# Packed products one half step later, from the third batch on, in a fused attention and feed-forward kernel

## The chip, the cores and the metric

One Trainium2 chip, one core of it. The metric is the device time of one launch in microseconds; the kernel before takes 954.0 us (median of 3 runs, 953.77 to 955.78). Lower is better.

## What is computed

Eight batches, 8 heads, 576 tokens, 64 columns a head, fp32. First an attention in two stages through 32 packed tokens, then a spectral mixing of its output and a feed-forward of width 2048:

```
s = 0.125 * p @ k.T ; a = softmax(s) ; p_packed = a @ v          # 32 x 64 a head
s = 0.125 * q @ p_packed.T ; a = softmax(s) ; x = a @ p_packed   # 576 x 64 a head
u  = x + real(fft(fft(x, axis=1), axis=2))                       # tokens, then 512 columns
un = (u - mean(u)) / sqrt(var(u) + 1e-6)
out = u + relu(un @ w_ch1) @ w_ch2
```

## The kernel before

The work has two halves that are laid into each other. `front(b)` computes `u` of one batch: it is a generator, cut by `yield` into pieces. `ffn` runs the feed-forward over a tile of four blocks of 128 tokens; there are nine tiles (0 to 8). During tile t the front of batch t+1 runs piece by piece between the matmuls of the feed-forward, and the last pieces of batch t (called `rest`: the tokens that a block has no place for, "the tokens apart", whose values are `px<-bd,fa`) run at its start.

A tile goes through 16 chunks j of the 2048 hidden columns. Each has an **up half** (12 matmuls of 512 columns into the PSUM buffer `ph`) and a **down half** (12 matmuls into `acc0` to `acc3`). After `ph` is full, ACT makes `hh` from it (relu, rounded high part, L964) and DVE makes `hl` (the low part, L965); both read `ph`. The down half that follows in the program belongs to the chunk before. Behind each half stands a call of `step(i)`:

```
up(j); step(2*j); down(j - 1); step(2*j + 1)
```

so that even steps stand behind an up half and odd steps behind a down half. `step` lets the next piece of `gen` (the front of the next batch) or of `rest` be issued there. On PE, DVE, ACT and POOL the instructions stand in the order in which this Python code issues them (a manual schedule); SP's DMAs are placed by the tool, save those that are pinned.

The pieces of a front and their order stand in `ORDER`, one string for batch 0, one for batch 1 and one for the others; `y` is a `yield`. Letters that matter here: S scores, D the scores sent to DRAM in blocks (`fare`) and back transposed (`e1T`, group 0 on SP's queue, group 1 on ACT's queue at step 2), X sums of the scores, p packed products (`po`), d transposes of the result (`pptp`, then `ppT`, `pph`, `ppl`), g spectrum of the packed values (`pg`, then `turned`), U queries against the packed keys (`s2Tt`, `s2T`), e subtraction of the maximum, m of the mean. The exponentials of e are issued one step after it, by `after(1, exps)` in `less_one`. A digit is the group of four heads, 0 or 1.

PSUM has eight buffers of 128 x 512: `acc0` to `acc3`, one named `ph`, three named `ps` that go round for all else. `queries(0, 1)` (L463) uses the buffer `ph` too, for the short tail of group 1:

```
tails = [bank("s2Tt")] + ([psf.tile([P, 512], F32, tag="ph", name="s2Tt")] if len(gs) == 2 else [])
```

`narrow` then issues the tails of both groups in turn (group 0 first), and the 512-wide parts after them. `packed(g)` (L425) multiplies `e1T` by the values and normalises with `rinv` on DVE (L439); `spread` on POOL makes `bd` of it. `Turned.send_next` sends a finished block of the next tile to DRAM and back, at the steps in `SENDS`, if its mean was taken in an earlier step.

Of the kernel before, what the change touches and what calls it, by code (L numbers as in the profile page):

```python
# [14 lines left out]
ALU = mybir.AluOpType  # L15
AX = mybir.AxisListType

P = 128
S = 576
HS = S // 2  # L20
D = 64
NPK = 32
# [19 lines left out]
         "i20 d1 w1 m0 q1 e1 T3 a0 f0 i120 g0 j0 r0 w2 w3 c0 w4 w5 i40 g1 m1 P0 w6 X0 j1 a1 f1 c1 r1 P1 X1 v2 W10 P2 w7 T2",  # L42
         "K0 K1 Q0 Q1 y S V0 V1 y X y p0 p1 y d0 d1 y g0 y U y g1 y e0 y e1 y y m0 y a0 y m1 y a1 y f0 y r0 y h0 y f1 y r1 y "
         "h1 y y",
         "V0 V1 S D y X Q0 Q1 y p0 p1 y d0 d1 y g0 y U y g1 y e0 y e1 y y m0 y a0 y m1 y a1 y f0 y r0 y h0 y f1 y r1 y "
         "h1 y y")


# [35 lines left out]
def tile_kernel(ctx, tc, kpT, qT, v, w1, w2, tabS, tabH, tabL, tabR, tabF, tabB, tabT, sel, ident_d, out):  # L84
    nc = tc.nc
# [14 lines left out]
    def bank(name):  # L100
        nbank[0] += 1
        if nbank[0] % 7 < 4 and spare:
            return psf.tile([P, 512], F32, tag=spare[nbank[0] % 7], name=name)
        return ps.tile([P, 512], F32, tag="ps", name=name)
# [115 lines left out]
    def load_weights(i):  # L220

        for _ in range(BITS[i]):
            bits(*topped.pop(0))
            fetch_free()
        for _ in range(TOPS[i]):
            tops(*coming.pop(0))
# [10 lines left out]
    now = {}  # L237
# [10 lines left out]
    def next_step():  # L248
        steps[0] = (steps[0] or 0) + 1
        for item in [x for x in due if x[0] <= steps[0]]:  # L250
            due.remove(item)
            item[1]()
# [39 lines left out]
    def front(b):  # L292
        kps, vts, qts, e1s, e1T, rinv, away = {}, {}, {}, {}, {}, {}, {}
# [8 lines left out]
        def in_place(kind, g, what):  # L302

            if b == 0:
                late[kind, g] = what
            else:
                what()
# [4 lines left out]
        def load_values(g):  # L312
            if b < 2:
                vt = load(v[b, :, g], [P, 5, 4 * D], "vt", (g, 4) if b == 0 else None, b == 1)
                vts[g] = [vt[:, c] for c in range(5)]
                return
            vt = load(v[b, :, g, 0:4], [P, 4, 4 * D], "vt", "wst", True)
            vts[g] = [vt[:, c] for c in range(4)]
            vts[g].append(load(v[b, :, g, 4], [P, 4 * D], "vt4", ("xh", "oh")[g], True))
# [51 lines left out]
        def chunk_rows(c):  # L371

            return P if c < 3 or b < 2 else P - 32
# [51 lines left out]
        def packed(g):  # L425

            if g not in vts:
                load_values(g)
            vt = vts[g]
            po = bank("po")  # L430
            for c in range(5):
                kk = chunk_rows(c)
                for h in range(4):
                    nc.tensor.matmul(  # L434
                        po[h * NPK:(h + 1) * NPK, :D], e1T[g][:kk, h, c, :],
                        vt[c][:kk, h * D:(h + 1) * D], start=(c == 0), stop=(c == 4),
                        tile_position=(0, h * NPK))
            pp2 = work.tile([P, 2, D], F32, tag="pp2", name="pp2")
            nc.vector.tensor_scalar(pp2, po[:, :D].unsqueeze(1).to_broadcast([P, 2, D]), rinv[g], None, ALU.mult)  # L439
            pp2s[g] = pp2  # L440

            def spread():
                mask, n = (bpair, 2) if b else (bmask, 4)
                bd[g] = work.tile([P, n, D], F32, tag=f"bd{n}", name="bd")
                nc.gpsimd.tensor_tensor(bd[g], pp2[:, 0:1, :].to_broadcast([P, n, D]), mask.unsqueeze(2).to_broadcast([P, n, D]),
                                        ALU.mult)

            in_place("b", g, spread)
# [158 lines left out]
        def folded_parts(g):  # L607
# [6 lines left out]

        parts = {"S": lambda _: scores(0, 1), "U": lambda _: queries(0, 1), "D": lambda _: scores_away(0, 1),
                 "s": scores, "t": turned_scores, "u": score_sums, "p": packed, "d": packed_parts, "q": queries, "e": less_one, "m": less_mean, "g": values_spectrum, "a": weights, "f": folded, "r": folded_rest,
                 "h": folded_parts, "c": copies,
                 "T": load_tables, "B": lambda _: load_turn(), "K": load_keys, "V": load_values,
# [173 lines left out]
        for t, base in enumerate((0, FO) if b else ()):  # L792
# [15 lines left out]
            h = work.tile([P, DM], F32R, tag="tmp", name="yr_h", bufs=3)  # L808
# [117 lines left out]
    def wsplits():  # L926

        for t, _ in enumerate(tiles):
            for n, j in [(0, 0)] + [x for j in range(1, NJ) for x in ((0, j), (1, j - 1))] + [(1, NJ - 1)]:
# [4 lines left out]
                yield  # L934

    def ffn(first, turned, step, nxt, alone):
        keys = turned.keys
        n = len(keys)
# [5 lines left out]
        def up(j, moves=(), between=lambda: None):  # L944
            moves = list(moves)
            wh, wl = ready.pop(0)

            pool, tag = (ps, "ps") if alone and j % 2 else (psf, "ph")
            ph = pool.tile([P, 512], F32, tag=tag, name="ph")

            step = T // 2 if first == 0 and j < SPL else T
            for t in (slice(i, i + step) for i in range(0, T, step)):
                for k in range(12):
                    if step < T:
                        c, (l, r) = k % 4, ((wh, uh), (wl, uh), (wh, ul))[k // 4]
                    else:
                        c, (l, r) = k // 3, ((wh, uh), (wh, ul), (wl, uh))[k % 3]
                    nc.tensor.matmul(ph[:, t], l[:, c * P:(c + 1) * P], r[:, c, t], start=(k == 0), stop=(k == 11))  # L958
                    if moves:
                        moves.pop(0)()  # L960
            between()
            hh = ffp.tile([P, 512], F32R, tag="hh", name="hh")
            hl = ffp.tile([P, 512], F32R, tag="hl", name="hl")
            nc.scalar.activation(hh[:, :T], ph[:, :T], AF.Relu)  # L964
            nc.vector.scalar_tensor_tensor(hl[:, :T], ph[:, :T], 0.0, hh[:, :T].bitcast(F32), ALU.max, ALU.subtract)  # L965
            return hh, hl
# [26 lines left out]
        for j in range(NJ):  # L993
# [13 lines left out]
            if nxt is not None and j == NJ - 2 and not nxt.sent:  # L1007
                less(0, 1)
            step(2 * j)
            sends(2 * j)  # L1010
            if nxt is None and j == NJ - 1:
# [77 lines left out]
    rest = gen0  # L1089
    for t, (first, tk) in enumerate(tiles):  # L1090

        gen = gens.pop(t + 1, None) or (front(t + 1) if t + 1 < B else iter(()))
        ended = []

        def step(i):

            next_step()
            if i == 2 and t + 1 < B and t:
                now.pop("back")()
            if i in ((1, 2) if t else (0, 2)):  # L1100
                next(rest, None)
            elif not ended and next(gen, None) == "rest":
                ended.append(gen)
            if t == 0:
                load_weights(i)
            assert i < 2 * NJ - 1 or t + 1 >= B or ended

        nxt = Turned(tiles[t + 1][1]) if t + 1 < len(tiles) else None

        with tc.manual_schedule(engines=MANUAL):  # L1110
            ffn(first, cur, step, nxt, t + 1 >= B)
        cur, rest = nxt, gen
# [114 lines left out]
```

## Time and profile before

| | |
|---|---|
| timed runs, median (range) | 954.0 us (953.77 to 955.78) |
| the profiled execution | 957.94 us, its span 956.1 us |
| mean granted TensorE clock | 0.994 |
| busy: PE, DVE, ACT, POOL | 940.9, 568.6, 444.5, 451.5 us |
| instructions | 15116 |

The profile is one execution, and it was longer than the timed runs. A busy time is the sum over the span in which an engine's datapath works; a row of the timeline has the start in us from the span's start, the duration in us, engine, line, operation, and what is written from what with shapes. A number in brackets behind a row is the time that the engine was idle before it, and what ended that. Matmuls are pipelined, so a row is longer than the distance to the next.

### The profile page before, as it was taken

The page shows a single profiled execution, that of the slowest core. Times are in us where ns is not written, and L with a number is a line of the kernel's source. Part 1 is how long each engine was busy: PE and PEld are TensorE (multiplying, and loading weights), DVE is VectorE, ACT ScalarE, POOL GpSimd, SP SyncE. Part 2 cuts the span into 40 slices and gives each one's busy share as a digit, 9 for nine tenths or more (in the row PEclk, how much of TensorE's full clock was granted, in tenths as well). Part 3 has the DMA queues.
Part 4 walks back from the last instruction along what each step waited for, and adds up shares of the span by engine and source line. Part 5 has one row for each costly group of instructions (what it writes and reads, how often), then busy time and mean ns, then how long its engine had stood idle before and what let it go on. Part 6 is the DMA issues. An engine that isn't in the chain of part 4 may idle for free.

```text
span 956.1 us, 15116 instructions
## 1 busy us (share of the span) xinstructions
PE 940.9 (98%) x5593; PEld 761.5 (80%) x5593; DVE 568.6 (59%) x1171; ACT 444.5 (46%) x909; POOL 451.5 (47%) x392
## 2 busy tenths in 40 slices
PE   8899999999999999999999999999999999999998
PEld 5678887788778887788778877888778878887886
DVE  6789866594648656684668476864668353123112
ACT  4698565434524444444534444454444443233231
POOL 4456444553445435543555354543554355444442
PEclk9899999999999999999999999999999999999999
DMA  9694226200440016200540045100610011001001
GB/s 353 239 328 132 68 88 194 81 1 1 150 142 26 1 46 210 85 1 24 167 149 1 1 133 176 55 1 23 212 34 19 20 48 45 23 23 45 1 0 45
DMA packets 49304, 81.00 MB, mean 85 GB/s; under 512 B 7120, under 2 KB 29136, under 8 KB 49232
## 3 DMA queue, kind: packets, MB, share of 16 engines
q1 hardware_dynamic: 42896, 69.82, 21.6%
q10 hardware_dynamic: 5328, 8.98, 2.9%
q0 software_dynamic: 1008, 1.25, 0.5%
q8 instruction: 44, 0.72, 0.3%
q14 instruction: 28, 0.23, 0.1%
HBM read 59.71 MB, written 20.32 MB: 84 GB/s over the span
## 4 chain that ended last, share of the span: by engine, by line
PE 93%; DVE 2%; DMA 2%; ACT 1%; POOL 1%; issue 1%; SPq 0%; ACTq 0%; DVEq 0%; POOLq 0%
PE acc L977 41%; PE ph L958 40%; PE px L693 2%; PE po L434 1%; DMA w1f<-w 1%; PE py L743 1%; DMA e1T<-fare 1%; PE py L289 1%; PE py L290 1%; PE py L288 1%; PE s2T L338 1%; PE s L338 0%; ACT e L365 0%; PE pz L635 0%; PE pz L658 0%
## 5 line engine op out<-in xcount | busy, mean ns | idle before, releaser
L110 POOL TENSOR_TENSOR wr_l<-w2f,wr_h 128x512 fp32r<-128x512 f32 x144 | 188.4, 1308 | 290.6 <-ACT wr_h L107 268.5
L110 POOL TENSOR_TENSOR wr_l<-w1f,wr_h 128x512 fp32r<-128x512 f32 x144 | 195.4, 1357 | 190.1 <-ACT wr_h L107 165.1
L965 DVE SCALAR_TENSOR_TENSOR hl<-ph,hh 128x512 fp32r<-128x512 f32 x144 | 99.5, 691 | 297.1 <-ACT hh L964 294.7
L977 PE MATMUL acc<-wr_h,hh 128*128 128x512 f32 x577 | 229.4, 398 | 0.0
L958 PE MATMUL ph<-uh,wr_h 128*128 128x512 f32 (+1 forms) x580 | 226.2, 392 | 1.0 <-ACT uh L107 1.0
L977 PE MATMUL acc<-wr_l,hh 128*128 128x512 f32 x577 | 226.3, 392 | 0.0
L977 PE MATMUL acc<-wr_h,hl 128*128 128x512 f32 x577 | 225.8, 391 | 0.0
L958 PE MATMUL ph<-ul,wr_h 128*128 128x512 f32 (+1 forms) x580 | 224.6, 389 | 0.5 <-DVE ul L110 0.5
L958 PE MATMUL ph<-uh,wr_l 128*128 128x512 f32 (+1 forms) x580 | 224.4, 389 | 0.0
L964 ACT ACTIVATE hh<-ph 128x512 fp32r<-128x512 f32 x144 | 86.1, 598 | 243.5 <-PE ph L958 243.2
L107 ACT CAST wr_h<-w1f 128x512 fp32r<-128x512 f32 x144 | 89.3, 620 | 185.2 <-POOL wr_l L110 80.3
L958 PEld LDWEIGHTS ph<-uh,wr_h 128*128 128x128 f32 x580 | 108.6, 188 | 29.0 <-DVE s L480 5.9
L977 PEld LDWEIGHTS acc<-wr_h,hh 128*128 128x128 f32 x577 | 108.8, 189 | 25.3 <-issue 1.6
L977 PEld LDWEIGHTS acc<-wr_h,hl 128*128 128x128 f32 x577 | 108.9, 189 | 23.1
L958 PEld LDWEIGHTS ph<-uh,wr_l 128*128 128x128 f32 x580 | 108.5, 188 | 22.6
L958 PEld LDWEIGHTS ph<-ul,wr_h 128*128 128x128 f32 x580 | 108.7, 188 | 21.9 <-DVE ul L110 1.0
L977 PEld LDWEIGHTS acc<-wr_l,hh 128*128 128x128 f32 x577 | 108.8, 189 | 21.1
L107 ACT CAST wr_h<-w2f 128x512 fp32r<-128x512 f32 x144 | 88.3, 613 | 33.1 <-PE acc L977 25.9
L1035 DVE SCALAR_TENSOR_TENSOR ubuf<-acc,stat,ubuf 128x512 f32<-128x512 f32 (+1 forms) x37 | 24.9, 731 | 2.1 <-PE acc L977 2.1
L262 ACT ACTIVATE junk<-ubuf,stat 128x512 f32<-128x512 f32 x36 | 25.8, 717 | 0.1
L266 POOL TENSOR_TENSOR stat<-stat,mhalf 128x1 f32<-128x1 f32 x36 | 25.7, 727 | 0.0
L613 DVE TENSOR_TENSOR fl<-f,fh 128x712 fp32r<-128x712 f32 x14 | 18.9, 1351 | 9.1 <-ACT fh L611 9.0
(222 smaller groups left out, 1084.7 us busy)
## 6 DMA issues: line engine op xcount, KB each, us to landing
kp<-kpT SPq DMA_DIRECT2D x16, 608.0 KB, 5.0
out<-ubuf SPq DMA_DIRECT2D x35, 256.0 KB, 3.9
far<-unt SPq DMA_DIRECT2D x28, 256.0 KB, 2.0
back<-far SPq DMA_DIRECT2D x112, 64.0 KB, 2.0
qt<-qT ACTq DMA_DIRECT2D x12, 576.0 KB, 5.1
vt<-v SPq DMA_DIRECT2D x12, 512.0 KB, 4.0
w1f<-w SPq DMA_DIRECT2D x9, 512.0 KB, 7.0
w2f<-w SPq DMA_DIRECT2D x9, 512.0 KB, 7.2
```

The lines of the kernel that those rows point to most:

```text
L107: copied = nc.scalar.copy(hi, src)
L110: (lo_eng or nc.vector).tensor_tensor(lo, src, hi.bitcast(F32), ALU.subtract)
L262: nc.scalar.activation(junk, u, AF.Square, bias=st[:, 1:2], scale=-sign, accum_out=st[:, 2:3])
L266: nc.gpsimd.tensor_tensor(st[:, 2:3], st[:, 2:3], mhalf, ALU.pow)
L288: nc.tensor.matmul(o, lh, rh, start=first, stop=False)
L613: nc.vector.tensor_tensor(fl[g], f, fh[g].bitcast(F32), ALU.subtract)
L693: nc.tensor.matmul(banks[r][rows, k * 256 + g * P:k * 256 + (g + 1) * P], x[g][at, w], bd[g][at].rearrange("p a d -> p (a d)"), start=True ...
L958: nc.tensor.matmul(ph[:, t], l[:, c * P:(c + 1) * P], r[:, c, t], start=(k == 0), stop=(k == 11))
L964: nc.scalar.activation(hh[:, :T], ph[:, :T], AF.Relu)
L965: nc.vector.scalar_tensor_tensor(hl[:, :T], ph[:, :T], 0.0, hh[:, :T].bitcast(F32), ALU.max, ALU.subtract)
L977: nc.tensor.matmul(acc[i][:, cols], l[:, w], r[:, cols], start=(j == 0 and k == 0), stop=(j == NJ - 1 and k == 2 and cols.stop == DM))
L1035: nc.vector.scalar_tensor_tensor(u[:, cols], acc[i][:, cols], stat_of[keys[i]][:, 2:3], u[:, cols], ALU.mult, ALU.add)
```

## The change

From the third batch on (b >= 2; tiles 1 to 6 carry such fronts):

- a `y` stands in front of `p0 p1`, so the packed products and all behind them come one half step later; a `y` behind `e1` goes, so that m0 and all behind it stay at their steps;
- both groups of the packed products go into one `ps` bank side by side, and are normalised after both;
- in every tile but the first, the last piece of `rest` (the values of the tokens apart) moves from step 2 to step 5, where it is issued ahead of the next piece of the front, which is `p0 p1`.

```
-         "V0 V1 S D y X Q0 Q1 y p0 p1 y d0 d1 y g0 y U y g1 y e0 y e1 y y m0 y a0 y m1 y a1 y f0 y r0 y h0 y f1 y r1 y "
+         "V0 V1 S D y X Q0 Q1 y y p0 p1 y d0 d1 y g0 y U y g1 y e0 y e1 y m0 y a0 y m1 y a1 y f0 y r0 y h0 y f1 y r1 y "
          "h1 y y")
...
-            po = bank("po")
+            if g == 0 or b < 2:
+                po = now["po"] = bank("po")
+            else:
+                po = now["po"]
+            po = po[:, g * D:(g + 1) * D]
...
-                        po[h * NPK:(h + 1) * NPK, :D], e1T[g][:kk, h, c, :],
+                        po[h * NPK:(h + 1) * NPK], e1T[g][:kk, h, c, :],
...
+            if b < 2:
+                normalized(g, po)
+            elif g == 1:
+                for k in range(2):
+                    normalized(k, now["po"][:, k * D:(k + 1) * D])
+
+        def normalized(g, po):
+
             pp2 = work.tile([P, 2, D], F32, tag="pp2", name="pp2")
-            nc.vector.tensor_scalar(pp2, po[:, :D].unsqueeze(1).to_broadcast([P, 2, D]), rinv[g], None, ALU.mult)
+            nc.vector.tensor_scalar(pp2, po.unsqueeze(1).to_broadcast([P, 2, D]), rinv[g], None, ALU.mult)
...
-            if i in ((1, 2) if t else (0, 2)):
+            if i in ((1, 5) if t else (0, 2)):
                 next(rest, None)
-            elif not ended and next(gen, None) == "rest":
+            if i not in ((1, 2) if t else (0, 2)) and not ended and next(gen, None) == "rest":
                 ended.append(gen)
```

`gen` isn't taken further at steps 1 and 2, as before. The pieces of the front then stand at: X Q 3, p 4 (now 5), d 5 (6), g0 6 (7), U 7 (8), g1 8 (9), e0 9 (10), e1 10 (11), m0 12 in both.

The order on PE in tile 3, at the packed products (`po`) and the values of the tokens apart (`px`). Before:

```order
L958 MATMUL ph<-uh,wr_l 128x512
L693 MATMUL px<-bd,fa 64x128 x4
L977 MATMUL acc_4034<-wr_h,hh 128x512
...
L958 MATMUL ph<-uh,wr_l 128x512
L434 MATMUL po<-vt,e1T 32x64 x16
L434 MATMUL po<-vt_4061,e1T 32x64 x4
L434 MATMUL po<-vt,e1T 32x64 x16
L434 MATMUL po<-vt_4065,e1T 32x64 x4
L977 MATMUL acc_4034<-wr_h,hh 128x512
```

And in the changed kernel (its lines are 12 higher from L450 on):

```order
L989 MATMUL acc_4035<-wr_h,hl 128x512
L705 MATMUL px<-bd,fa 64x128 x4
L438 MATMUL po<-vt,e1T 32x64 x16
L438 MATMUL po<-vt_4059,e1T 32x64 x4
L438 MATMUL po<-vt,e1T 32x64 x16
L438 MATMUL po<-vt_4063,e1T 32x64 x4
L970 MATMUL ph<-uh,wr_h 128x512
```

The values moved from behind an up half to directly ahead of the products, and both now stand behind a down half.

The order on PE in tile 3 at the queries (`s2Tt`, the tails, and `s2T`). Before:

```order
L977 MATMUL acc_4037<-wr_h,hh 128x512
L977 MATMUL acc_4037<-wr_l,hh 128x512
L977 MATMUL acc_4037<-wr_h,hl 128x512
L338 MATMUL s2Tt<-qt,ppT 32x64 x8
L338 MATMUL s2T<-qt,ppT 32x512 x8
L958 MATMUL ph<-uh,wr_h 128x512
```

And in the changed kernel:

```order
L970 MATMUL ph<-uh,wr_h 128x512
L970 MATMUL ph<-ul,wr_h 128x512
L970 MATMUL ph<-uh,wr_l 128x512
L338 MATMUL s2Tt<-qt,ppT 32x64 x8
L338 MATMUL s2T<-qt,ppT 32x512 x8
L989 MATMUL acc_4032<-wr_h,hh 128x512
```

The queries moved from behind a down half to behind an up half.

The order on DVE in tile 1 around the transposes of the queries, which read `s2Tt` and `s2T`. Before:

```order
L965 SCALAR_TENSOR_TENSOR hl<-ph,hh 128x512
L529 TENSOR_TENSOR turned<-pg,turn 128x516 x2
L535 TENSOR_TENSOR turned<-turned 128x258 x2
L480 STREAM_TRANSPOSE s_2157<-s2Tt 128x64
L480 STREAM_TRANSPOSE s_2156<-s2Tt 128x64
```

And in the changed kernel:

```order
L541 TENSOR_TENSOR turned<-pg,turn 128x516 x2
L547 TENSOR_TENSOR turned<-turned 128x258 x2
L977 SCALAR_TENSOR_TENSOR hl<-ph,hh 128x512
L492 STREAM_TRANSPOSE s_2166<-s2Tt 128x64
L492 STREAM_TRANSPOSE s_2165<-s2Tt 128x64
```

An `hl` now stands directly ahead of the transposes, where two sums of the spectrum stood.

## Rows read from the trace of the kernel before

**Rows 1.** The page: span, busy time and share of the engines, and the granted clock of TensorE in 40 slices, in tenths.

```profile
span 956.1 us, 15116 instructions
...
PE 940.9 (98%) x5593; PEld 761.5 (80%) x5593; DVE 568.6 (59%) x1171; ACT 444.5 (46%) x909; POOL 451.5 (47%) x392
...
PEclk9899999999999999999999999999999999999999
```

**Rows 2.** The waits of PE, longest first: engine, what waited, for what; us in total, times, longest us.

```profile
PE py L743 <- POOL f L592: 2.1, 1, 2.1
PE po L434 <- DMA e1T<-fare: 1.8, 1, 1.8
```

**Rows 3.** Timeline of PE in tile 2, packed products to the transposes behind them.

```profile
268.36 0.77 PE L434 MATMUL po<-vt,e1T 128*32 128x64 f32 x40
270.89 0.77 PE L434 MATMUL po<-vt,e1T 128*32 128x64 f32 x40 [1.76 <-DMA e1T<-fare]
271.59 0.66 PE L977 MATMUL acc<-wr_h,hh 128*128 128x512 f32 x1
...
276.04 0.38 PE L454 MATMUL pptp<-ident,pp 128*128 128x128 f32 x2
```

**Rows 4.** Two stretches in tile 2: start and end, length, busy us of PE, PEld, DVE, ACT and POOL (with instructions), then the granted clock, the DMA share and GB/s.

```profile
268.36:271.77 3.41, 1.65 (x82) 1.42 (x82) 1.00 (x3) 1.10 (x2) 1.95 (x3) 1.00 0.83 324
271.77:275.19 3.41, 3.41 (x9) 2.65 (x10) 1.40 (x3) 0.00 (x0) 0.57 (x1) 0.50 0.22 85
```

**Rows 5.** The chain that ended last, in tile 2: start, us, what.

```profile
266.14 4.35 DMA e1T<-fare
270.49 0.40 issue
```

**Rows 6.** Timeline of PE in tile 3, last matmul of an up half, packed products, down half, transposes, first matmul of the next up half.

```profile
375.33 0.39 PE L958 MATMUL ph<-uh,wr_l 128*128 128x512 f32 x1
375.79 1.33 PE L434 MATMUL po<-vt,e1T 128*32 128x64 f32 x80
377.05 0.50 PE L977 MATMUL acc<-wr_h,hh 128*128 128x512 f32 x1
...
379.94 0.38 PE L454 MATMUL pptp<-ident,pp 128*128 128x128 f32 x2
380.07 0.48 PE L958 MATMUL ph<-uh,wr_h 128*128 128x512 f32 x1
```

**Rows 7.** Timeline of PE, ACT and DVE behind three up halves. First the next work of PE, hh, the weight split behind it and hl in tile 3; then hl behind the up half of rows 6; then the next work of PE and hl in tile 2.

```profile
382.90 0.28 PE L521 MATMUL pg<-basis,pph 128*128 128x258 f32 x1
383.16 0.60 ACT L964 ACTIVATE hh<-ph 128x512 fp32r<-128x512 f32 x1 [1.51 <-PE ph L958]
383.66 0.61 ACT L107 CAST wr_h<-w2f 128x512 fp32r<-128x512 f32 x1
383.80 0.69 DVE L965 SCALAR_TENSOR_TENSOR hl<-ph,hh 128x512 fp32r<-128x512 f32 x1 [0.67 <-ACT hh L964]
...
376.38 0.69 DVE L965 SCALAR_TENSOR_TENSOR hl<-ph,hh 128x512 fp32r<-128x512 f32 x1 [1.84 <-ACT hh L964]
...
292.28 0.39 PE L977 MATMUL acc<-wr_h,hh 128*128 128x512 f32 x1
293.45 0.69 DVE L965 SCALAR_TENSOR_TENSOR hl<-ph,hh 128x512 fp32r<-128x512 f32 x1 [1.24 <-ACT hh L964]
```

**Rows 8.** Timeline of PE in tile 2, around the values of the tokens apart.

```profile
261.57 0.39 PE L958 MATMUL ph<-ul,wr_h 128*128 128x512 f32 x1
261.80 0.39 PE L958 MATMUL ph<-uh,wr_l 128*128 128x512 f32 x1
262.11 0.65 PE L693 MATMUL px<-bd,fa 64*64 64x128 f32 x8
262.70 0.50 PE L977 MATMUL acc<-wr_h,hh 128*128 128x512 f32 x1
263.04 0.40 PE L977 MATMUL acc<-wr_l,hh 128*128 128x512 f32 x1
```

**Rows 9.** All hh and all hl of the span: count, duration in ns (min/median/max), first and last start.

```profile
L964 ACT ACTIVATE hh<-ph x144: 577/598/614, 47.9 to 946.4; 128x512 fp32r<-128x512 f32 x144
...
L965 DVE SCALAR_TENSOR_TENSOR hl<-ph,hh x144: 652/692/698, 48.5 to 947.0; 128x512 fp32r<-128x512 f32 x144
```

**Rows 10.** Timeline of DVE and PE in the first batch: a copy, and the matmuls that waited for it.

```profile
11.40 0.29 DVE L456 COPY ppT<-pptp 128x128 f32<-128x128 f32 x1 [0.42 <-PE pptp L454]
...
11.75 0.32 PE L338 MATMUL s2Tt<-w1f,ppT 64*32 64x64 f32 x8 [0.38 <-DVE ppT L456]
```

**Rows 11.** Timeline of PE in tile 3, the queries' wide parts and the next up half.

```profile
386.37 1.06 PE L338 MATMUL s2T<-qt,ppT 64*32 64x512 f32 x16
387.37 0.50 PE L958 MATMUL ph<-uh,wr_h 128*128 128x512 f32 x1
```

**Rows 12.** Timeline of ACT and DVE in tile 3: the squares of the tokens apart, both normalisations, and the high and low part of the packed values of group 0.

```profile
374.48 0.72 ACT L262 ACTIVATE junk<-ubuf,stat 128x512 f32<-128x512 f32 x1
...
377.05 0.60 DVE L439 TENSOR_SCALAR pp<-po,ri 128x128 f32<-128x128 f32 x2
...
380.57 0.27 ACT L107 CAST pph<-pptp 128x128 fp32r<-128x128 f32 x1
380.87 0.29 DVE L110 TENSOR_TENSOR ppl<-pptp,pph 128x128 fp32r<-128x128 f32 x1 [0.33 <-ACT pph L107]
```

## The prediction

> **What bounds the kernel now.** I read the page first: TensorE's share of the span and its granted clock [rows 1]. PE is busy for 940.9 of 956.1 us at full clock nearly throughout, so a saved microsecond of another engine is worth nothing unless PE waited for it, and every wait that is put on PE adds to the end. Then the list of PE's waits, longest first [rows 2]: the first, 2.1 us for a fold of the first batch, lies ahead of the tiles; the second is 1.8 us for scores that come back by DMA, and it is the one wait inside the tiles. Then the timeline of PE around that wait, in tile 2 [rows 3], the clock beside it [rows 4], the chain through it [rows 5] and the same place one tile later [rows 6]. Last I looked, on PE, ACT and DVE together, for whatever the moved pieces will newly meet: the end of an up half, where the bank "ph" is emptied [rows 7].
>
> **The DMA wait.** In tile 2 the packed products begin at 268.36, stop after the first group, and the second group starts at 270.89, after 1.76 us without work [rows 3]; the chain goes through the last return of e1T, which lands 0.40 us before that [rows 5]. From 271.77 to 275.19 the granted clock is 0.50, the lower of the two levels (1.2 GHz), after 1.00 in the stretch before [rows 4], so most of the down half behind the wait runs at half speed. In tile 3 the same two pieces run without trouble: packed products from 375.79 to 377.05, 1.26 us, down half to 379.94, 2.89 us [rows 6]. Tile 2 took 271.59 - 268.36 = 3.23 and 276.04 - 271.59 = 4.45 us [rows 3], so the wait with what the clock took cost 1.97 + 1.56 = 3.53 us. Tile 3 is just late too: its last up matmul starts at 375.33 and the products at 375.79, 0.46 us, where an interruption otherwise takes 0.31 [rows 6, 8], 0.15 us more. Together 3.7 us. With the products one half step (2.7 us) later, behind the down half, the second group in tile 2 would be asked for near 268.36 + 2.8 for the down half + 0.59 for the values [rows 8] + 0.63 for the first group (half of 1.26) = 272.4, some 1.5 us after the start that the data allowed. So 3.7 us of the profiled execution go. But this execution took 957.94 us and the median of the timed runs is 954.0: the 3.9 us between them are about this wait, so I take it that the timed runs mostly don't have it, and that it gives them nothing.
>
> **One interruption fewer.** A short piece put between full-width matmuls costs more than its own time. Around the values of the tokens apart, the step from the last up matmul to the piece is 0.31 us instead of 0.23, and the first step behind it is 0.34: 0.08 + 0.11 = 0.19 us [rows 8]. Now these 8 rows stand directly in front of the packed products, in tiles 1 to 6. One such pair goes, and one step from values to products comes, which the trace doesn't show: nothing at best, a full 0.19 at worst. The saving is 0 to 0.19 us a tile; I take the middle, 0.10, for both ends are equally near: 6 x 0.10 = 0.6 us, bounds 0 and 1.1. The Trainium skill, in TensorEngine Tiling (Array Packing), section Tiling Modes, says that a change of tiling mode drains the engine; values (64 x 64) and products (128 x 32) are two modes, so by it the new step isn't free and the saving would lie below the upper bound.
>
> **The queries land on a bank that is still being read.** This is the largest term. Everything behind the packed products moves one half step with them, so the queries (s2Tt, s2T) move from step 7 to step 8. Odd steps stand behind a down half, even steps behind an up half, as the order on PE shows. The tail of the second group is written into the only buffer "ph". At step 7 that buffer had been written one down half ago and emptied meanwhile. At step 8 it has just been filled, and the second matmul of the piece has to wait until ACT has made hh and DVE has made hl from it; in the order of DVE, hl now stands directly in front of the transposes of s2Tt. How long that is stands in tile 3: the first matmul behind the up half starts at 382.90, hh starts at 383.16, hl runs from 383.80 for 0.69 us and ends at 384.49 [rows 7], 1.59 us later. Both instructions are steady: hh 577 to 614 ns, hl 652 to 698 ns over 144 of each [rows 9]. From an end on DVE to the start of the matmul that waited for it takes 0.06 us (11.69 to 11.75, [rows 10]). PE takes matmuls in order, so the rest of the queries and the whole down half queue behind it: 1.65 us a tile, in tiles 1 to 6, 9.9 us. Nothing hides it, for PE has no slack. Below: the earliest end of hl in these rows is 376.38 + 0.69 - 375.79 = 1.28 us behind the up half, where PE itself came late [rows 6, 7]: 1.34 x 6 = 8.0. Above: where DVE or ACT came late, hl ended at 293.45 + 0.69 - 292.28 = 1.86 us [rows 7]: 1.92 x 6 = 11.5. I take 1.65, since that row is also the end of an up half with a short piece behind it. What the queries free in exchange is small: the next up half no longer follows directly on the transposes of s2Tt, but it didn't wait for them (s2T takes 1.00 us to the next up half, 386.37 to 387.37, the length of its own work, [rows 11]).
>
> **What else moves, at no cost on PE.** Both products share a bank and are normalised together: 0.60 us of DVE for the two [rows 12], behind DVE's sums of the tokens apart, which now stand there too; the transposes of the result come a whole up half later (380.07 to 382.90 is one, 2.83 us [rows 6, 7]), and that hides it. If it didn't, the transposes at step 6 would wait. Means: the exponentials of a group are issued one step before its means are taken, and have that half step on ACT; the steps from m0 on stay where they were. On SP the turned block of the tokens apart is sent at step 12 instead of 4 or 5 in tiles 1 and 3; it is split in the last steps, and behind it in that queue stand keys for the next tile. If that cover were gone, SP's transfers would come a few us later and still before the tile's end. The weight splits on POOL now pass the spread of the packed values one step later; they run a whole half step ahead of PE.
>
> **The sum.** Against the profiled execution: 957.94 - 3.7 - 0.6 + 9.9 = 963.5 us. Against the timed median, without the DMA wait: 954.0 - 0.6 + 9.9 = 963.3 us. I forecast 963.4 us. Its own ends are 954.0 - 1.1 + 8.0 = 960.9 and 954.0 + 11.5 = 965.5.
>
> **The rivals.** First, the clock falls after each new wait, as it did after the 1.76 us in tile 2 [rows 4]. Then the 1.56 us that it cost there come six times: 963.4 + 9.4 = 972.8 us; one, two or three times, 965.0 to 968.1. For it speaks that the new wait is nearly as long. Against it speaks the neighbourhood: in tile 2 the thin packed products lay on both sides of the wait and PE was busy for 1.65 of 3.41 us [rows 4], while now dense up matmuls end directly before it. The Trainium skill, in TensorE: Matmul & The Clock Gate, section "A second HAM failure mode: psum-queue depth-cycling", tells of a kernel that went round its PSUM banks and whose short idle times were enough to swing the clock between the levels; by that rule the time would be the 972.8 us above. No tile of this trace shows such a bank wait.
>
> Second, another wait comes beside it. At step 6 ACT now has hh, a weight split, the squares of the tokens apart and then the parts of the packed values, which the spectrum at step 7 multiplies. From the rows: hh from 0.26 us after the up half, the split from 0.76 to 1.37 [rows 7], squares 0.72 and, from the start of a part to the end of its low part on DVE, 380.87 + 0.29 - 380.57 = 0.59 [rows 12]: ready 2.7 us after the up half. PE comes there after two transposes, 0.13, and a down half of some 2.83, at 2.96 [rows 6, 7]. In tiles 1, 3 and 5, which have these squares, 0.3 us are left. If ACT comes a split (0.61 us) later, PE waits 0.3 us three times: 964.3 us.
>
> Third, on the other side: the new wait is short and the old one is worth its price in the timed runs too. This takes an hl that is done 0.93 us sooner than rows 7 say, since (3.7 + 0.6) / 6 = 0.72 us of wait a tile is the point at which it turns. Without any wait and with the DMA wait gone it would be 954.0 - 4.3 = 949.7 us, without the DMA wait in the timed runs 953.4. For it speaks that one timed run was 955.78, so waits of that kind come and go; against it, that hh and hl are two instructions in a chain, 0.58 + 0.65 = 1.23 us at their shortest [rows 9].
>
> **How the numbers follow.** Forecast 0.70, clock 0.15, second wait 0.07, other side 0.08. About 0.2% (1.9 us) is what a measurement of this kernel can tell from no change. The first three are slower by more than that: 0.92; the last is split evenly, 0.04 faster and 0.04 the same. The range goes from 960.5, just under the forecast's own lower end, to 969.6, which takes in a clock that falls after up to four of the six waits (963.4 + 4 x 1.56); outside stay the other side and the fullest clock cases, together some 0.15.
>
> **What would show it.** In the changed profile: the wait of the packed products for the DMA is gone, and they take 1.3 us in every tile; a wait of s2Tt for hl stands at the top of PE's list, 6 times, about 1.6 us each, always behind an up half; clock 1.00 in the tiles. The values of the tokens apart run straight into the products. If s2Tt doesn't wait, or waits under 0.7 us, the largest term is wrong; if low clock stands behind these waits, the first rival has it.

## The result and the profile after

The changed kernel takes 961.46 us (median of 6 runs, 961.2 to 961.98) against 954.12 us (6 runs, 953.36 to 955.78): ratio 1.007, 95% interval 1.006 to 1.008; by the medians it is 7.3 us slower. Forecast were 963.4 us, with 960.5 to 969.6 as the range.

The page of the changed kernel, to be read beside [rows 1]: the span grew by 3.1 us though PE is busy 2.8 us less. It grew by less than the timed 7.3 us because the profiled execution of the kernel before was a long one (957.94 us, with the DMA wait); that of the changed kernel took 961.2, as the timed ones do.

```profile
span 959.2 us, 15122 instructions
...
PE 938.1 (98%) x5593; PEld 760.1 (79%) x5593; DVE 566.4 (59%) x1171; ACT 444.4 (46%) x909; POOL 456.0 (48%) x392
...
PEclk9999999999999999999999999999999999999999
```

A 9 in the clock's row stands for 90% or more, so a fall of 3.4 us in a slice of 24 would not show in it. The stretch of a whole tile tells more (columns as in [rows 4]); here is tile 4:

```profile
467.30:571.88 104.58, 103.33 (x642) 83.86 (x641) 68.40 (x142) 46.72 (x98) 49.51 (x40) 1.00 0.24 78
```

The granted clock is 1.00, and so it is in the stretches of the tiles 1 to 3, 5 and 6; for the kernel before, the stretch of tile 2, with the fall of [rows 4] in it, shows 0.98.

PE's list of waits, beside [rows 2] (what waited, for what; us in total, times, longest):

```profile
PE s2Tt L338 <- DVE hl L977: 7.5, 6, 1.2
PE py L755 <- POOL f L604: 2.2, 1, 2.2
```

A wait that the kernel before did not have stands at the top, six times, once in each of the tiles 1 to 6. The wait of `po` for the DMA is gone from the list.

The queries in tile 3 on PE, ACT and DVE, beside [rows 7, 11]:

```profile
386.50 0.39 PE L970 MATMUL ph<-uh,wr_l 128*128 128x512 f32 x1
386.82 0.30 PE L338 MATMUL s2Tt<-qt,ppT 64*32 64x64 f32 x2
386.98 0.60 ACT L976 ACTIVATE hh<-ph 128x512 fp32r<-128x512 f32 x1 [2.85 <-PE ph L970]
387.61 0.69 DVE L977 SCALAR_TENSOR_TENSOR hl<-ph,hh 128x512 fp32r<-128x512 f32 x1 [1.48 <-ACT hh L976]
388.36 0.28 PE L338 MATMUL s2Tt<-qt,ppT 64*32 64x64 f32 x7 [1.25 <-DVE hl L977]
...
389.49 0.50 PE L989 MATMUL acc<-wr_h,hh 128*128 128x512 f32 x1
```

Read it downward: the tail of group 0 starts at 386.82, that of group 1 writes `ph` and has to wait for hl, which ends at 388.30; PE goes on at 388.36 and reaches the down half at 389.49. From 386.82 to 389.49 are 2.67 us. In the kernel before the same piece took 1.13, from its tails' row, here, to the up half at 387.37 of [rows 11]:

```profile
386.23 0.34 PE L338 MATMUL s2Tt<-qt,ppT 64*32 64x64 f32 x16
```

So the wait costs 1.54 us, though the list shows 1.25 for it: the list counts from the end of the matmul before.

The values of the tokens apart and the packed products, tile 4, beside [rows 6, 8]:

```profile
480.04 0.39 PE L989 MATMUL acc<-wr_h,hl 128*128 128x512 f32 x1
480.36 0.65 PE L705 MATMUL px<-bd,fa 64*64 64x128 f32 x8
480.94 1.34 PE L438 MATMUL po<-vt,e1T 128*32 128x64 f32 x80
482.21 0.50 PE L970 MATMUL ph<-uh,wr_h 128*128 128x512 f32 x1
```

Values 0.58 us and products 1.27 us, each as long as it was when it stood alone in front of a full-width matmul (0.59 in [rows 8], 1.26 in [rows 6]); the step from one to the other costs nothing more than that.

The length of a tile is the quickest measure of all that follows: from the first score matmul of tile 4 to that of tile 5, on PE. In this pair of tiles the profiled execution of the kernel before had no DMA wait. Before:

```profile
467.87 0.34 PE L338 MATMUL acc<-kp 64*32 64x64 f32 x15
...
571.14 0.34 PE L338 MATMUL acc<-kp 64*32 64x64 f32 x16
```

After:

```profile
467.30 0.32 PE L338 MATMUL acc<-kp 64*32 64x64 f32 x12
...
571.88 0.34 PE L338 MATMUL acc<-kp 64*32 64x64 f32 x15
```

103.27 us have become 104.58: 1.31 us more, which is 1.54 for the wait less 0.23 for the interruption saved (e3 below measures the 0.23 by itself). Six such tiles make 7.9 us.

### The profile page after: what moved, and what is told of

Same layout as the page of the kernel before. It is cut to its first block, busy times and chain, and to the rows that moved or that the text cites. A ratio compares the mean times of both kernels' runs of the same rounds, so it can differ in the third digit from the quotient of the medians.

```text
span 959.2 us, 15122 instructions
## 1 busy us (share of the span) xinstructions
PE 938.1 (98%) x5593; PEld 760.1 (79%) x5593; DVE 566.4 (59%) x1171; ACT 444.4 (46%) x909; POOL 456.0 (48%) x392
## 3 DMA queue, kind: packets, MB, share of 16 engines
q0 software_dynamic: 1008, 1.25, 0.5%
## 4 chain that ended last, share of the span: by engine, by line
PE 94%; DVE 2%; ACT 1%; DMA 1%; POOL 1%; issue 0%; SPq 0%; DVEq 0%; ACTq 0%; POOLq 0%
PE ph L970 41%; PE acc L989 41%; PE px L705 2%; PE po L438 1%; DMA w1f<-w 1%; PE py L289 1%; PE py L288 1%; PE py L290 1%; PE py L755 1%; PE s2T L338 1%; PE s L338 1%; PE pz L670 0%; DVE hl L977 0%; PE pz L647 0%; ACT hh L976 0%
## 5 line engine op out<-in xcount | busy, mean ns | idle before, releaser
L110 POOL TENSOR_TENSOR wr_l<-w1f,wr_h 128x512 fp32r<-128x512 f32 x144 | 199.2, 1383 | 185.3 <-ACT wr_h L107 158.0
L541 DVE TENSOR_TENSOR turned<-pg,turn 128x516 f32<-128x516 f32 x32 | 20.6, 688 | 11.7 <-PE pg L534 11.6
```

The costliest lines, as they stand in the source:

```text
L110: (lo_eng or nc.vector).tensor_tensor(lo, src, hi.bitcast(F32), ALU.subtract)
L541: nc.vector.tensor_tensor(x, pg[:, :N2].unsqueeze(1).to_broadcast([P, 2, N2]), w, ALU.mult)
```

## The experiments

All were timed in turn with the kernel before on their chip; the ratio is the one to compare, since its median there lay between 954.6 and 955.3 us. Where two rows are set against each other in microseconds, it is by what each lost to its own kernel before, by the medians. The tile is the one measured above.

| run | tile 4, us | time, us | ratio to before (95%) |
|---|---|---|---|
| kernel before | 103.27 | 954.12 | 1 |
| the change | 104.58 | 961.46 | 1.007 (1.006 to 1.008) |
| e1, queries at step 9 | 104.56 | 961.23 | 1.0071 (1.0058 to 1.0083) |
| e3, values at step 2 | 104.81 | 963.40 | 1.0090 (1.0076 to 1.0104) |
| e4, before, queries at step 8 | 104.82 | 963.45 | 1.0093 (1.0077 to 1.0109) |
| e6, wide parts first | 103.72 | 957.35 | 1.0023 (1.0014 to 1.0032) |
| e7, queries at step 7 | 103.03 | 953.06 | 0.9981 (0.9972 to 0.9990) |
| e8, e7 with values at step 2 | 103.26 | 954.53 | 0.9992 (0.9982 to 1.0001) |
| e9, before, values at step 4 | 103.67 | 957.11 | 1.0028 (1.0017 to 1.0040) |
| e10, e1 with gl on DVE | 107.74 | 977.54 | 1.0235 (1.0215 to 1.0255) |
| e11, before, values at 4, one bank | 103.04 | 954.52 | 0.9995 (0.9986 to 1.0004) |
| e12, the change with two banks | 104.66 | 964.52 | 1.0102 (1.0088 to 1.0116) |

**The place of the queries alone (e4).** One string of the kernel before is edited:

```
-         "V0 V1 S D y X Q0 Q1 y p0 p1 y d0 d1 y g0 y U y g1 y e0 y e1 y y m0 ..."
+         "V0 V1 S D y X Q0 Q1 y p0 p1 y d0 d1 y g0 y g1 y U y e0 y e1 y y m0 ..."
```

> The kernel before with one edit: the second spectrum at step 7 and the queries at step 8, behind an up half; packed products, values and means stay where they were. Theory: the wait for the bank comes alone, 6 x 1.54 = 9.2 us, 954.1 + 9.2 = 963.3 us. Rival (the loss comes from the late products): 954.1 us.

963.45 us, a tile of 104.82 (1.55 over), and PE's list has the new wait and no other in the tiles 1 to 6:

```profile
PE s2Tt L338 <- DVE hl L965: 7.5, 6, 1.2
```

The rival that late products cost by themselves falls: here they stand where they stood, and the loss is all there (8.1 us over the kernel before by the medians; 9.2 were expected).

**The wait made shorter (e6).** The wide parts of the queries are issued ahead of the tails (`wide` is true for the queries from the third batch on):

```
-            for c, w in ((1, slice(512, S)), (0, slice(0, 512))):
+            parts = ((1, slice(512, S)), (0, slice(0, 512)))
+            for c, w in reversed(parts) if wide else parts:
```

> The changed kernel with the 512-wide parts of the queries issued ahead of the tails, from the third batch on. Theory (the tail waits until hl has read ph): the wide parts, 0.99 us, run while hl is made, the wait falls from 1.54 to about 0.55 us, 6 x 0.99 = 5.9 us go: 955.5 us. Rival (the queries wait for something that comes with the step, such as the spectrum's banks or the packed values): the wide parts wait as the tails did, 961.5 us.

PE in tile 3:

```profile
385.71 1.09 PE L339 MATMUL s2T<-qt,ppT 64*32 64x512 f32 x16
386.60 0.27 PE L339 MATMUL s2Tt<-qt,ppT 64*32 64x64 f32 x2
387.25 0.34 PE L339 MATMUL s2Tt<-qt,ppT 64*32 64x64 f32 x14 [0.39 <-DVE hl L978]
387.52 0.50 PE L990 MATMUL acc<-wr_h,hh 128*128 128x512 f32 x1
```

The wide parts, in other banks, start at once, and the tail of group 1 still waits, now 0.39 us by its row: it is the bank `ph` that is waited for, nothing that the step brings. The piece takes 1.81 us instead of 2.67, 0.86 less (0.99 expected; the tails, issued last, now take longer at the end). A tile of 103.72 says the same. The run is 2.1 us over its kernel before where the change was 7.3 over, a gain of 5.3 us, as six times 0.86 = 5.2 asks; 5.9 were expected.

**The queries behind a down half again, later (e1).** In the changed kernel:

```
-         "... d0 d1 y g0 y U y g1 y e0 y e1 y m0 ..."
+         "... d0 d1 y g0 y g1 y U y e0 y e1 y m0 ..."
```

> The changed kernel with the queries one half step later again (step 9, behind a down half) and the second spectrum ahead of them at step 8. Theory (the loss is the wait of the queries' tail for the bank ph, and nothing else): the wait of s2Tt for hl is gone from PE's list, and 6 x 1.54 = 9.2 us go from 961.5, to 952.2 us, faster than the kernel before. Rival (the loss comes from the packed products and all behind them being late, wherever the queries stand): about 961 us, since here the queries are later still.

This missed. The queries no longer wait, as expected, but the time is that of the change, and so the number of the rival. The rival does not have it all the same: e4 above lost the time without late products, and e7 below has late products without the loss. PE's list names another wait:

```profile
PE ph L970 <- DVE s L492: 9.1, 6, 1.5
```

The up half behind the queries fills `ph` next, and it waits for DVE's transposes of the tail. PE, DVE and POOL in tile 4:

```profile
494.55 0.34 PE L338 MATMUL s2Tt<-qt,ppT 64*32 64x64 f32 x16
...
497.24 0.47 PE L970 MATMUL ph<-uh,wr_h 128*128 128x512 f32 x1 [1.50 <-DVE s L492]
```

```profile
494.04 2.90 DVE L547 TENSOR_TENSOR turned<-turned 128x258 f32<-128x258 f32 x2
496.86 0.37 DVE L492 STREAM_TRANSPOSE s<-s2Tt 128x64 f32<-128x64 f32 x2
```

```profile
493.92 1.30 POOL L110 TENSOR_TENSOR gl<-turned,gh 128x516 fp32r<-128x516 f32 x1
495.18 1.47 POOL L110 TENSOR_TENSOR wr_l<-w1f,wr_h 128x512 fp32r<-128x512 f32 x1
```

The two sums of the spectrum ahead of the transposes take 2.90 us (1.47 and 1.52, overlapping), with POOL at work without a gap beside them; the durations over all of them (count, shortest/median/longest in ns) are

```profile
L547 DVE TENSOR_TENSOR turned<-turned x28: 414/544/1522, 69.2 to 704.6; 128x258 f32<-128x258 f32 x28
```

and 420 to 430 ns over all in the kernel before. So the bank has two ends, and this order freed the one and shut the other. The theory stands in what it said of the queries' wait, and was too narrow in holding that nothing else could stop PE there.

**Is it POOL's work that slows the sums? (e10)** e1 with `TL = (0, 0, 1)`: the low parts `gl` of the later batches go from POOL to DVE.

> The run with the queries at step 9, with the low parts of the spectra (gl) made on DVE instead of POOL from the third batch on. There the sums of the second spectrum on DVE took 1.49 and 1.52 us beside POOL's work without a gap, 0.43 elsewhere, and the tail's transposes behind them came late. Theory (a DVE sum of two operands in SBUF is slow while POOL works): the sums fall to some 0.5 us, the wait of the up half for the transposes from 1.5 us to under 0.5 in spite of DVE's added 0.8, and the time falls by 5 us or more from 961.2. Rival (the transposes are late because of the place behind the spectrum): the wait grows by the added work to 2.3 us, 966 us.

977.54 us: neither theory's time. DVE in tile 4:

```profile
500.19 1.38 DVE L110 TENSOR_TENSOR gl<-turned,gh 128x516 fp32r<-128x516 f32 x1 [0.34 <-ACT gh L107]
501.49 1.28 DVE L541 TENSOR_TENSOR turned<-pg,turn 128x516 f32<-128x516 f32 x2
502.81 1.33 DVE L547 TENSOR_TENSOR turned<-turned 128x258 f32<-128x258 f32 x2
504.83 0.70 DVE L110 TENSOR_TENSOR gl<-turned,gh 128x516 fp32r<-128x516 f32 x1 [0.69 <-ACT gh L107]
```

The sums fell from 2.90 to 1.33 us with less work on POOL, and the same `gl` takes 1.38 us at 500.19, where POOL made a weight split (499.71 to 501.01), and 0.70 at 504.83, where POOL was idle. POOL beside them:

```profile
499.71 1.30 POOL L110 TENSOR_TENSOR wr_l<-w2f,wr_h 128x512 fp32r<-128x512 f32 x1 [2.65 <-ACT wr_h L107]
502.23 1.29 POOL L110 TENSOR_TENSOR wr_l<-w1f,wr_h 128x512 fp32r<-128x512 f32 x1 [1.21 <-ACT wr_h L107]
```

So a DVE operation with both operands in SBUF was slow beside POOL's work: the theory's mechanism held. Its time did not, because both `gl` came to stand on DVE ahead of what PE waits for: that of the first group ahead of the products of the spectrum, whose banks the wide parts of the queries need, and that of the second, which waits for ACT, ahead of the tail's transposes. PE in tile 4:

```profile
501.60 0.34 PE L338 MATMUL s2Tt<-qt,ppT 64*32 64x64 f32 x16
502.23 1.69 PE L338 MATMUL s2T<-qt,ppT 64*32 64x512 f32 x16 [0.29 <-DVE turned L541]
505.83 0.47 PE L970 MATMUL ph<-uh,wr_h 128*128 128x512 f32 x1 [1.92 <-DVE s L492]
```

From the tails to the up half are 4.23 us, where e1 took 2.69 (494.55 to 497.24): 1.54 more, and between 1.50 and 1.54 in the other tiles, 9.1 us in all six. The wait of the up half grew to 1.9 us, and behind the wait in tiles 1 and 4 the clock went down (columns as in [rows 4]):

```profile
503.60:507.06 3.46, 1.54 (x12) 1.05 (x6) 2.73 (x7) 0.62 (x1) 0.00 (x0) 1.00 0.58 167
507.07:510.47 3.40, 3.40 (x10) 2.63 (x9) 0.00 (x0) 0.13 (x1) 0.00 (x0) 0.50 0.48 198
```

The fall in tile 4 cost 1.6 us (the tile took 107.74 us, the tiles 3 and 5, at full clock, 106.08 and 106.15). With as much for the other fall and the 9.1 that is 12.3 of the 12.9 us by which the profiled execution (974.14 us) is longer than that of e1 (961.23). The median is 3.4 us longer still, at a mean granted clock of 0.989 where the profiled one had 0.992; more falls of the clock would do that, but no trace shows them.

**One interruption fewer (e3).** The changed kernel with the values back at step 2:

```
-            if i in ((1, 5) if t else (0, 2)):
+            if i in ((1, 2) if t else (0, 2)):
```

> The changed kernel with the values of the tokens apart back at step 2, not in front of the packed products. Theory (an interruption fewer saves 0.22 us a tile, 1.3 us in all): 961.5 + 1.3 = 962.8 us. Rival (what the changed kernel won back, some 1.9 us, is the DMA wait that the timed runs of the kernel before also had): 961.5 us, since the products stay late.

The scores of tile 4 and of tile 5:

```profile
467.82 0.29 PE L338 MATMUL acc<-kp 64*32 64x64 f32 x8
...
572.63 0.29 PE L338 MATMUL acc<-kp 64*32 64x64 f32 x8
```

A tile of 104.81, 0.23 over the change. The time does not decide: 8.1 us over its kernel before, where the change was 7.3 over, lies between the theory (1.3 more) and the rival (nothing more), and the intervals of the two ratios overlap. So it is the tile that speaks for the theory.

**Values in front of the products, without the rest (e9).** The kernel before with `(1, 4)` in that line, and the `if` of the change in place of the `elif` behind it.

> The kernel before with one edit: the values of the tokens apart at step 4, directly in front of the packed products, which stay where they were. Theory: a clean tile takes 103.05 us, 6 x 0.22 = 1.3 us go, and the products come 0.6 us later than before, which takes a part of the DMA waits: 1.3 to 2.3 us faster. Rival (the step from values to products costs as much as the pair that goes): no change.

Slower by 2.5 us, a miss for both. PE's list says why:

```profile
PE po L434 <- DVE xa L714: 2.7, 6, 0.6
```

The two banks of the values and one of the first products are all three `ps` banks; the products of group 1 take the bank of the values and wait until DVE has read it (`xa`), behind an hl.

**Both groups in one bank (e11, e12).** e11 is e9 with the products' part of the change, so the kernel before with all of the change but the shift of half a step; e12 is the change with a bank for each group (`if g == 0 or b < 2` made always true, the second normalisation taking each group's own).

> The kernel before with two parts of the change alone: the values of the tokens apart directly in front of the packed products (at step 4, where the products stood), and both groups of products in one bank; the order of the front is that of before, so the queries stay at step 7. Theory (the wait of the products for xa in the run with values at step 4 came from a fourth bank out of three; one bank for both groups takes it away): no wait of po for xa, a clean tile of 103.05 us, 1.3 us less than the kernel before and up to 0.6 more for the DMA wait: ratio 0.998. Rival (the products wait because they stand directly behind the values): the wait of 0.65 us a tile stays, ratio 1.003 as in that run.

The wait for `xa` is gone and tile 4 takes the 103.04 us expected, but the gain in time is not to be told from none: 0.9995 (0.9986 to 1.0004). In tiles 1 to 3 the products took 1.82, 1.91 and 1.59 us instead of 1.27, waiting for the DMA; that is 1.5 us together, as much as the 1.4 us (six times 0.23) that the interruption gives:

```profile
164.89 0.77 PE L438 MATMUL po<-vt,e1T 128*32 128x64 f32 x40 [0.36 <-DMA e1T<-fare]
```

> The changed kernel with one part undone: each group of packed products has its own bank again. Theory: the second group waits for DVE's reading of the values, 0.65 us in tiles 1 to 6, in addition to the wait of the queries: 3.9 us over the change, ratio 1.012 to the kernel before. Rival (sharing the bank is of no account): ratio 1.007 to 1.008 as the change.

964.52 us, ratio 1.0102: 9.5 us over its kernel before where the change was 7.3 over, so some 2.2 us more; 3.9 were expected. The wait comes back, but in three of the six tiles only (tile 4, in the table, is not one of them):

```profile
PE po L439 <- DVE xa L727: 1.4, 3, 1.0
```

At step 5 no hl stands directly ahead of `xa`, so DVE is often in time. So the shared bank is worth some 2 us to the change, less than e9 made expect.

**The queries at step 7 behind late products (e7, e8).** The order is

```
"V0 V1 S D y X Q0 Q1 y y p0 p1 y E y U y g0 y e0 y g1 y e1 y m0 ..."
```

where E is d for both groups with both plain copies (`ppT`) ahead of the splits; the squares of the tokens apart come one step later. Both spectra stand at even steps, as in the kernel before.

> The changed kernel with the queries at step 7, behind a down half: order p at 5, transposes of both groups with both plain copies first at 6, queries 7, first spectrum 8, e0 9, second spectrum 10, e1 11, means as before; squares of the tokens apart one step later. Theory: no wait of PE in the tiles, 0.22 us a tile saved by the values in front of the products, the DMA wait gone: a clean tile takes 103.05 us where before had 103.27 and the change 104.6, and the time is 1.3 us and the timed DMA waits (some 0.6 to 1.5 us) under that of the kernel before: 2 to 3 us faster. Rival (moving the products late costs by itself): as slow as the change, 7 us over.

953.06 us, ratio 0.9981 (0.9972 to 0.9990), a tile of 103.03: this version beats both kernels, the one before by 1.5 us, where 2 to 3 were expected. The scores of tile 4 and of tile 5:

```profile
464.44 0.29 PE L339 MATMUL acc<-kp 64*32 64x64 f32 x8
...
567.47 0.29 PE L339 MATMUL acc<-kp 64*32 64x64 f32 x8
```

PE's list has no wait in the tiles 1 to 6, and all 28 sums of the spectra take 419 to 430 ns again.

> As the run before, but the values of the tokens apart stay at step 2. Theory: a clean tile takes 103.27 us as before the change; what is left of a gain is the DMA wait of the timed runs alone, 0.6 to 1.5 us under the kernel before. Rival (the timed runs have no DMA wait, as the prediction took it): the same time as the kernel before, within 0.3 us.

A tile of 103.26, as in the kernel before; the time, 0.9992 (0.9982 to 1.0001), does not tell theory and rival apart, for the interval holds both. So the DMA wait is worth between nothing and 1.7 us in a timed run, if nothing else in this order costs or saves.

## Why the prediction was right

**The bank.** Right in place, cause and sign, shown by e4 and e6: 1.54 us a tile for 1.65 forecast. (PE's list shows 1.25 for each where the prediction named 1.6 as the sign; that is the way the list counts, as said above.) The difference of 0.1 is a double count. A thin piece of 64 x 32 begins 0.32 us behind the last up matmul (386.50 to 386.82); the spectrum in [rows 7], at 382.90, began 0.22 us behind its own:

```profile
382.68 0.39 PE L958 MATMUL ph<-uh,wr_l 128*128 128x512 f32 x1
```

In both cases hh starts 0.48 us behind that matmul. So it starts only 0.16 us after the piece here and 0.26 there, and the time that an interruption takes in any case was counted in the wait as well.

**The interruption.** Mis-sized: 0.23 us a tile (e3 against the change, e7 against e8, e11 against the kernel before), for 0.10 with 0.19 as the upper bound. The step from values to products, taken as half of an interruption, costs nothing, and the bound itself was short, since [rows 8] show only the first step behind the piece: in tile 4 of the kernel before the down half behind the values takes 2.85 us (473.36 to 476.21) where one directly behind an up half in tile 5 takes 2.72 (602.65 to 605.37), 0.13 more, of which the first step has 0.11. The Trainium skill's rule that a change of tiling mode drains the engine (TensorEngine Tiling (Array Packing), Tiling Modes) shows no price of its own at this step: from the start of the values to what follows them are 0.58 us before products of another mode, and 0.59 in [rows 8] before a full-width matmul, which is a change of mode too. The prediction took from the rule that the saving would lie below the upper bound; it measured above it.

**The DMA wait.** Right that it goes: no such wait in the changed profile. That the timed runs mostly didn't have it is not refuted: the profile of e4, with the products at their old step, shows none, and that of e11 shows short ones in three tiles, so it comes and goes. 7.9 us in the tiles less the 7.3 measured leaves some 0.6 us for it, which is within the scatter, and e8 bounds it at 1.7. It is not quite the one wait inside the tiles, as the prediction had it: both kernels have another of 0.5 us in front of an up half of the last tile (`ph` for `ul`), which the change doesn't touch.

**The sum.** With the measured terms: 954.1 + 6 x (1.54 - 0.23) = 962.0, less what DMA waits the timed runs had; measured were 961.46. Both errors went the same way, 0.7 us for the bank and 0.8 for the interruption, and made 1.4 of the 1.9 us by which the forecast was high; the rest is too small to be told from scatter.

**The rivals.** The clock did not fall: the granted clock is 1.00 in every tile of the change, and of e1, e3, e4, e6 and e12, with bank waits of 0.4 us (e6) to 1.5 us (e1) in their rows. The swing between the levels of which the Trainium skill tells (TensorE: Matmul & The Clock Gate, "A second HAM failure mode: psum-queue depth-cycling") did not come in these runs; in e10, where the up half waited 1.9 us in each of the six tiles, the clock went to 0.50 behind two of the waits. That the dense up matmuls in front of the wait are what kept the clock up, as the prediction argued, no run tests. The second wait did not come: the first spectrum waits nowhere. The other side fell with the 1.54 us.

## What to carry to other kernels

When a whole group of pieces is shifted by a slot, look up for each piece which buffers are free in the new slot, not only whether its inputs come in time: here the other pieces moved well and the queries landed where the only buffer it could use had just been filled. A buffer that two users share has two ends, the reader that must be done before the piece and the one that must be done after it; check both, with what stands ahead of each on its engine. Price a wait from the row of the last instruction before it, not from a neighbour's start, so that the cost of the switch isn't counted twice.

## What the hardware showed unexpectedly

Sums of two SBUF operands on DVE (128 x 258, fp32) took 0.42 us with POOL idle (in tile 3 of the kernel before, from 385.72, between POOL's splits, which end at 385.65 and start at 386.87) and 1.47 to 1.52 beside POOL's uninterrupted work in e1; there the products with one operand in PSUM kept their times (680 to 696 ns over all 32). The Trainium skill has this in SBUF — State Buffer, section Who interferes with whom: a DVE instruction with two SBUF inputs contends with POOL's reads of SBUF; the trace agrees, with a factor of 3.5 here.
